# Products of C with the state on four tiles of 32 rows and 64 columns, in a chunked linear attention with two gated layers

## Chip, cores, metric

One core of one Trainium2 chip. The metric is the device time of one execution in microseconds; lower is better. Times that are shown for a kernel are the median of several executions, and one more execution was profiled.

## What is computed

x is [4, 8, 768, 32] (batch, heads, tokens, width), a is [4, 8, 768], B and C are [4, 8, 768, 16]. Cut to what matters, with chunks of tokens (the reference takes 32, the kernel 128; the result is the same sum):

```python
cum = cumsum(log(clip(a)))                          # in a chunk
L = exp(cum[i] - cum[j]) * (i >= j)
y_intra = ((C_i . B_j) * L) @ x                     # in a chunk
y_inter = (C @ state) * exp(cum)                    # from the chunks before
y = y_intra + y_inter
state = exp(sum(log_a)) * state + sum_j decay_j * B_j x_j
h = (sigmoid(y @ w_gate) * (y @ w_val)) @ w_out     # 256 -> 1536 -> 256
g = h @ w2_in                                       # 256 -> 2048
out = (g * sigmoid(g)) @ w2_out                     # 2048 -> 256
```

There is a state of 16 by 32 for each of the 8 heads of each batch. y of all heads, 256 wide, goes into the two gated layers, 3072 tokens in all.

## The kernel before, in words

The tokens are cut into 24 chunks of 128 (six for each batch), and the first gated layer takes them in blocks of 2, 2, 4, 4, 4, 4 and 4 chunks. The attention of later chunks is spread, in small steps, between the products of the first layer: `slot_steps(s)` (L407) lists what the attention does while chunk s is finished, and the loop at L642 takes some steps from the list after each gate, each value and each output product. While block b runs, the attention of block b+1 is computed. The order of the instructions of each engine is not written out: a planner sets it ahead of time from the order of the program and from the times that it reckons for each instruction, except for SyncE's queue, whose order is the program's. A tile with one buffer may be written anew once everything that reads its old content is done.

For a chunk q, with N = 16, D = 32, L = 128 tokens:

- `at_L` (L287) scans the decays on VectorE; `at_cb` (L321) makes C B in two halves of four heads (bank `cb`), and VectorE multiplies them by L (L337).
- `at_bw` (L297), on GpSimd, scales B and C by their decays into `bw` and `cw`. `at_cwT` (L312) transposes `cw` on TensorE into a bank `misc` (L317), and ScalarE copies it to SBUF (L319): `cwT`, [(head, n), token].
- `at_state` (L360) makes the sum of B x for a chunk: four pairs of heads, each a column tile of 32 columns (L368), into the same bank `misc`; VectorE adds it to the running state S2, [(head, n), (parity of the head, d)] (L377). `at_state2` (L382) writes the state as a block-diagonal matrix of 128 by 256 (L389), with zeros where row and column are of different heads.
- `at_y` (L339) builds y transposed, [(head, d), token], in one bank `y`, heads 0 to 3 in its columns 0 to 127 and heads 4 to 7 in columns 128 to 255. First come the two products of C with the state: for each half a full 128 by 128 tile of the block-diagonal matrix against `cwT` (L346); they start the sum. Then the eight products x L, one for each head, on a tile of 32 columns each (L352), four side by side. Chunks 0, 6, 12 and 18 start a batch and have no state product.
- `at_yT` (L395) splits y into hi and lo: a copy on ScalarE (L404), a subtraction on VectorE (L405), 256 columns each.

All of these are float32 products, which the trace shows as two records of weights and two of matmul each; the first layer's products (L462, L511) have tiles of 128 by 128 and 512 columns moving. In slots from 9 on, `joint` (L421) issues y of chunk s, both halves, then the transpose and the state sums of chunk s+1. PSUM has eight banks: three for gate and value, two for the first layer's sums, and one each for `misc`, `cb` and `y`.

After the attention its memory holds the second layer's weights, which are converted while the last block of the first layer runs (L676 to L678). At the start, `blk` (L100 to L103), a mask of 128 by 8, is made on GpSimd.

Of the kernel before, what the change touches and what calls it, by code (L numbers as in the profile page):

```python
# [8 lines left out]
F32 = mybir.dt.float32  # L9
# [9 lines left out]

# Tokens per block of the first gated layer, in chunks of 128.  # L20
BLOCKS = [2, 2, 4, 4, 4, 4, 4]
LAG = 2
# The first chunks, whose C B products take the short way through the tensor engine.
NX = 4
LB = 4
GV = 3
# Hidden blocks whose w_out is still whole for the first two blocks of tokens.
NAT = 7
# [5 lines left out]
def tile_linattn_moe_moe(  # L34
# [12 lines left out]
):  # L47
    """Decayed linear attention in chunks of 128, then two gated layers.

    float32 products run as float32r: an operand is split exactly into hi + lo  # L50
    (12 significant bits each) and hi*hi + hi*lo + lo*hi are summed in PSUM.
    The intra-chunk products split into three bfloat16 parts instead.

    The weights come as the raw 64-bit words of float64 and are rounded to float32
    (to nearest) on the chip.
    """
    nc = tc.nc
    nb, H, S, D = x.shape
    N = B.shape[-1]
# [13 lines left out]

# [1 line left out]
    wp = ctx.enter_context(tc.tile_pool(name="wp", bufs=1))  # L75
# [16 lines left out]

# [1 line left out]
    warm = wp.tile([P, 1], F32, name="warm")  # L94
# [3 lines left out]
    make_identity(nc, ident)  # L98
    # blk[(h n), h'] = 1 where h' == h
    blk = ap_.tile([P, H], F32, name="blk")  # L100
    nc.gpsimd.memset(blk, 1.0)
    nc.gpsimd.affine_select(blk, blk, [[-N, H]], ALU.is_ge, 0.0, base=0, channel_multiplier=1)
    nc.gpsimd.affine_select(blk, blk, [[N, H]], ALU.is_ge, 0.0, base=N - 1, channel_multiplier=-1)  # L103
    # eye[j, (h i)] = 1 where i == j
    eye = ap_.tile([P, H * L], BF16, name="eye")
    eye3 = eye.rearrange("p (h l) -> p h l", h=H)
    nc.vector.memset(eye, 1.0)
    nc.gpsimd.affine_select(eye3, eye3, [[0, H], [-1, L]], ALU.is_equal, 0.0, base=0, channel_multiplier=1)
    # sel[p, m] = 1 where p == L - 1
    sel = ap_.tile([P, P], F32, name="sel")  # L110
    nc.gpsimd.memset(sel, 1.0)
    nc.gpsimd.affine_select(sel, sel, [[0, P]], ALU.is_ge, 0.0, base=-(L - 1), channel_multiplier=1)

# [1 line left out]
    # exp of a sum of logs is a product: every decay is a running product of the  # L115
    # clipped a, which a scan over the tokens gives.
    def split(hi, lo, src):
        nc.scalar.copy(hi, src)
        nc.vector.tensor_sub(lo, src, hi.bitcast(F32))

# [1 line left out]
    # For each 128 of the hidden columns: hi and lo of [gate 2 x 128 | val 2 x 128 | out 256].  # L122
    w1 = w1p.tile([P, NF1, 2, 3 * DM], F32R, name="w1")
    cnt = 0

    def conv(raw, hi, lo, n, whole=None):
        """Raw float64 words [.., 2] -> float32, rounded to nearest, -> hi + lo;
        the last of them stay whole, if whole is given for them."""
        nonlocal cnt
        cnt += 1  # L130
        v = raw.rearrange("p (n t) -> p n t", t=2)
        t = stg["p"].tile([P, stg["n"]], F32, tag="cvt", name=f"cvt{cnt}", bufs=stg["cvt"])
        f, ti, r = t[:, :n], t[:, :n].bitcast(I32), v[:, :, 0]
        # The high word read as float32, times 2**-112, has the exponent field that
        # the float32 has after a shift by three bits; the sign is put back.
        nc.scalar.activation(f, v[:, :, 1].bitcast(F32), AF.Copy, scale=2.0**-112)
        nc.scalar.activation(r, v[:, :, 0].bitcast(U32), AF.Copy, scale=2.0**-29)
        nc.vector.tensor_scalar(ti, ti, 3, None, op0=ALU.logical_shift_left)  # L138
        nc.vector.scalar_tensor_tensor(  # L139
            ti, v[:, :, 1], -(2**31), ti, op0=ALU.bitwise_and, op1=ALU.bitwise_or  # L140
        )
        if whole is not None:
            n -= whole.shape[-1]
            nc.gpsimd.tensor_tensor(whole.bitcast(I32), ti[:, n:], r[:, n:], ALU.add)
            f, ti, r = f[:, :n], ti[:, :n], r[:, :n]
        nc.gpsimd.tensor_tensor(ti, ti, r, ALU.add)  # L146
        nc.scalar.copy(hi, f)
        nc.vector.tensor_sub(lo, f, hi.bitcast(F32))  # L148

    def load_w(w, f, ins, outs, native=None):  # L150
        """What the hidden columns f of a layer need of its weights."""
        nonlocal cnt
# [24 lines left out]
    def w1_split(f0, f1):  # L177
        """The whole w_out -> hi + lo."""
        for f in range(f0, f1):
            hi, lo = w1[:, f, 0, 2 * DM :], w1[:, f, 1, 2 * DM :]  # L180
            nc.scalar.copy(hi, whole(f))
            nc.vector.tensor_sub(lo, whole(f), hi.bitcast(F32))
# [3 lines left out]

# [1 line left out]
    T = [dict() for _ in range(NQ + 8)]  # L188

    def top(t):  # L190
        """The high halves of float32 words, as bfloat16."""
        return t.bitcast(BF16).rearrange("p (n t) -> p n t", t=2)[:, :, 1]
# [42 lines left out]
    def at_wide1(q):  # L235
# [7 lines left out]
        nc.scalar.copy(t["bT"], ps[:, :P])  # L243
        # C transposed, a copy for each head with zeros for the others
        t["cT"] = x1T[0][:, q % 2, q // 2 * H * L : (q // 2 + 1) * H * L].rearrange("p (h l) -> p h l", h=H)
# [19 lines left out]
    def at_bc3(q, which):  # L265
        """Parts 11122233 of B against parts 12312312 of C along the contraction."""
        t = T[q]
# [19 lines left out]
    def at_L(q):  # L287
        """L[j, h, i] = product of a over j < k <= i; 1 at i == j, 0 before.

        The scan restarts at i = 0, where a is replaced by 0."""  # L290
        t = T[q]
# [20 lines left out]
    def at_cwT(q):  # L312
        t = T[q]
        if q % NCH == 0:
            return
        ps = ps_at.tile([P, 512], F32, tag="misc", name=f"cwT{q}")
        nc.tensor.transpose(ps[:, :P], t["cw"].rearrange("p h n -> p (h n)"), ident)  # L317
        t["cwT"] = ap_.tile([P, P], F32, tag="cwT", name=f"cwT{q}", bufs=2)
        nc.scalar.copy(t["cwT"], ps[:, :P])  # L319

    def at_cb(q, half):  # L321
# [15 lines left out]
        nc.vector.tensor_mul(sl, ps, sl)  # L337

    def at_y(q, part):  # L339
        """y transposed, [(h d), i]: a head's 32 rows are a column tile."""  # L340
        t = T[q]
        if part == 0:
            t["y"] = ps_at.tile([P, KM, L], F32, tag="y", name=f"y{q}", bufs=1)
# [12 lines left out]

    # The state of a pair of heads, [(h n), (h' d)]: a column tile of 32 rows.
    S2 = ap_.tile([P, 2 * D], F32, name="S2")

    def at_state(q):  # L360
        b, c = divmod(q, NCH)
        t = T[q]
        if c == NCH - 1:
            return
        ps = ps_at.tile([P, 512], F32, tag="misc", name=f"st{q}")
        for p in range(H // 2):
            o = 2 * N * p
            nc.tensor.matmul(  # L368
                ps[o : o + 2 * N, : 2 * D],
                t["bw"][:, 2 * p : 2 * p + 2].rearrange("p h n -> p (h n)"),  # L370
                t["x"][:, 2 * p : 2 * p + 2].rearrange("p h d -> p (h d)"),
                start=True, stop=True, skip_group_check=True,
            )
        if c == 0:
# [7 lines left out]
    def at_state2(q):  # L382
        """The state as a block-diagonal matrix, [(h n), (h d)]."""
        t = T[q]
        if q % NCH == NCH - 1:
            return
        t["S"] = ap_.tile([P, DM], F32, tag="S", name=f"S{q}", bufs=2)
        sh = [P, H // 2, 2, D]
        nc.vector.tensor_mul(  # L389
# [5 lines left out]
    def at_yT(q):  # L395
        t = T[q]
        b, i = blk_of[q]
        if i == 0:
# [3 lines left out]
            ]  # L402
        hi, lo = (v[:, :, i * L : (i + 1) * L] for v in xT[b])
        nc.scalar.copy(hi, t["y"])  # L404
        nc.vector.tensor_sub(lo, t["y"], hi.bitcast(F32))  # L405

    def slot_steps(s, q0=0, q1=NQ):  # L407
        """What the attention does while chunk s is finished, as small steps;
        of chunks q0 to q1 only."""
        ok = lambda q: q0 <= q < q1  # L410
# [36 lines left out]

# [1 line left out]
    acc = {}  # L449
# [44 lines left out]
    def m1_out(b, f):  # L494
        n = BLOCKS[b] * L
        # Two blocks of at most 256 tokens can be under way, each in a bank.
        small = n <= 256
# [22 lines left out]

# [1 line left out]
    sp_order = ExitStack()  # L522
# [24 lines left out]

    # e_i[i, c, u]: the decay from the start of chunk c to its token i
    e_sb = first
# [10 lines left out]

    # dec[(h n), (c b)]: the decay over a whole chunk
    nc.tensor.matmul(
# [21 lines left out]

    # The weights are converted as the first two blocks run, these in turns.
    seen = set()
# [34 lines left out]

# [1 line left out]
    NA = 4  # L623
# [71 lines left out]

# [1 line left out]
    o2p = ctx.enter_context(tc.tile_pool(name="o2p", bufs=1))  # L697
# [93 lines left out]
    for o in queue_o[:-1]:  # L791
        m2_out(*o)
    # The last sums end one after the other, not all at once.
    with tc.manual_schedule(engines={mybir.EngineType.PE}):
# [32 lines left out]
```

## Time and profile before

| what | us |
|---|---|
| median of 3 executions | 680.7 (680.61 to 682.51) |
| span of the profiled execution, which is also the time on record for it | 680.8 |
| TensorE (matmul) busy | 647.7, 95% |
| TensorE (weight loads) busy | 524.9, 77% |
| VectorE busy | 436.0, 64% |
| ScalarE busy | 329.0, 48% |
| GpSimd busy | 109.3, 16% |

The span runs from the first to the last instruction. Busy times of different engines overlap, and the records of TensorE overlap each other as well: a matmul lasts longer than the distance to the start of the next. Line numbers are those of the kernel before. PE is TensorE, PEld its weight loads, DVE VectorE, ACT ScalarE, POOL GpSimd, SP SyncE.

### The profile page before, as it was taken

Reading aid. Unit: us, or ns where it says so; the run is one execution under the profiler, and the core shown is the slowest. Engines: PE = TensorE matmul, PEld = TensorE weight load, DVE = VectorE, ACT = ScalarE, POOL = GpSimd, SP = SyncE. Lnnn points to the kernel's source line nnn. Section 1 sums busy time; section 2 is a strip of 40 time slices with the busy share of each in tenths; the row PEclk is TensorE's granted clock in tenths of the full one; section 3 lists DMA queues with packets and bytes.
Section 4 is the critical chain, followed back from the end, with each engine's and each line's share of the span. In section 5 each row is a group of like instructions: output and inputs, shape, how many; then the busy total and the mean of one; then the engine's idle time right before and its main releaser. Section 6 shows DMA issues by size and latency. Waiting matters only on the chain.

```text
span 680.8 us, 10010 instructions
## 1 busy us (share of the span) xinstructions
PE 647.7 (95%) x3728; PEld 524.9 (77%) x3728; DVE 436.0 (64%) x658; ACT 329.0 (48%) x647; POOL 109.3 (16%) x128
## 2 busy tenths in 40 slices
PE   5689787999999999999999999999999999999997
PEld 2368676777777777777787888888888888888887
DVE  8987977767666758756689345464564555644544
ACT  5566634544444545435476335454454544534443
POOL 3534612212222313121133000000000000000000
PEclk9889989899999999999999999999999999999999
DMA  8935578867466375643132000000000000000000
GB/s 206 265 122 170 117 126 146 148 135 126 99 114 148 71 138 125 101 79 124 44 123 82 1 0 1 1 15 17 1 32 1 1 31 1 31 1 1 32 1 31
DMA packets 160592, 51.18 MB, mean 75 GB/s; under 512 B 119008, under 2 KB 156896, under 8 KB 160544
## 3 DMA queue, kind: packets, MB, share of 16 engines
q1 hardware_dynamic: 160544, 50.55, 33.4%
q8 instruction: 29, 0.48, 0.3%
q14 instruction: 19, 0.16, 0.1%
HBM read 36.80 MB, written 3.24 MB: 59 GB/s over the span
## 4 chain that ended last, share of the span: by engine, by line
PE 80%; DVE 6%; DMA 3%; issue 2%; POOL 2%; ACT 1%; SPq 1%; DVEq 0%; ACTq 0%; POOLq 0%
PE h L462 20%; PE acc L511 12%; PE v L462 12%; PE g L462 12%; PE o L739 11%; PE o L750 7%; PE o L745 2%; PE y L352 2%; PE cb L335 1%; DMA raw<-in_moe_w_out_dram 1%; DVE cvt L139 1%; PE y L346 1%; POOL cvt L146 1%; DVE cvt L138 1%; DVE w2b L148 1%
## 5 line engine op out<-in xcount | busy, mean ns | idle before, releaser
L462 PE MATMUL g<-xT,w 128*128 128x512 f32 (+1 forms) x504 | 124.2, 377 | 4.9 <-DVE sg L483 4.3
L462 PE MATMUL v<-xT,w 128*128 128x512 f32 (+1 forms) x504 | 121.7, 373 | 0.1
L462 PE MATMUL h<-x2T,w2b 128*128 128x512 f32 x432 | 113.3, 395 | 0.0
L719 DVE TENSOR_TENSOR sh<-h,sh 128x512 f32<-128x512 f32 x96 | 66.3, 691 | 69.6 <-ACT sh L718 69.0
L462 PEld LDWEIGHTS g<-xT,w 128*128 128x128 f32 x504 | 88.3, 193 | 24.3 <-DVE sg L483 5.5
L724 DVE TENSOR_TENSOR gl<-sh,gh 128x512 fp32r<-128x512 f32 x96 | 65.9, 691 | 55.5 <-ACT gh L456 31.9
L462 PEld LDWEIGHTS v<-xT,w 128*128 128x128 f32 x504 | 87.3, 191 | 17.0 <-issue 1.0
L511 PE MATMUL acc<-gh,w 128*128 128x512 f32 (+1 forms) x280 | 95.5, 384 | 1.6 <-ACT x1T L519 1.4
L718 ACT ACTIVATE sh<-h 128x512 f32<-128x512 f32 x96 | 57.7, 601 | 80.7 <-PE h L462 76.1
L462 PEld LDWEIGHTS h<-x2T,w2b 128*128 128x128 f32 x432 | 76.5, 188 | 15.2
L456 ACT CAST gh<-sh 128x512 fp32r<-128x512 f32 x96 | 59.2, 620 | 60.1 <-DVE sh L719 53.8
L456 ACT CAST gh<-sg 128x512 fp32r<-128x512 f32 (+1 forms) x70 | 41.2, 589 | 89.7 <-DVE sg L483 89.6
L739 PE MATMUL o<-w2b,gh 128*128 128x512 f32 x240 | 75.4, 395 | 0.0
L483 DVE TENSOR_TENSOR sg<-v,sg 128x512 f32<-128x512 f32 (+1 forms) x84 | 51.0, 607 | 30.0 <-PE v L462 29.8
L492 DVE TENSOR_TENSOR gl<-sg,gh 128x512 fp32r<-128x512 f32 (+1 forms) x70 | 50.1, 716 | 28.6 <-ACT gh L456 28.4
L295 DVE TENSOR_TENSOR_SCAN L<-L,eye 128x1024 f32<-128x1024 f32 x24 | 55.2, 2301 | 14.9 <-DMA L<-ac_d 14.6
L475 ACT ACTIVATE sg<-g 128x512 f32<-128x512 f32 (+1 forms) x84 | 44.9, 535 | 39.0 <-PE g L462 36.0
L511 PEld LDWEIGHTS acc<-gh,w 128*128 128x128 f32 x280 | 52.1, 189 | 13.1 <-ACT x1T L519 1.8
L750 PE MATMUL o<-w2b,gl 128*128 128x256 f32 x288 | 60.1, 280 | 0.0
L511 PE MATMUL acc<-gl,w 128*128 128x512 f32 (+1 forms) x140 | 53.9, 385 | 4.9 <-DVE gl L492 4.9
L146 POOL TENSOR_TENSOR cvt<-cvt,raw 128x512 int32<-128x512 int32 (+1 forms) x28 | 46.7, 1671 | 65.4 <-DVE cvt L139 50.6
L750 PEld LDWEIGHTS o<-w2b,gl 128*128 128x128 f32 x288 | 49.1, 188 | 4.9
(94 smaller groups left out, 784.9 us busy)
## 6 DMA issues: line engine op xcount, KB each, us to landing
L<-ac_d SPq DMA_DIRECT2D x23, 512.0 KB, 4.9
raw<-in_moe_w_out_dram SPq DMA_DIRECT2D x28, 256.0 KB, 3.7
raw<-in_moe_w_in_dram SPq DMA_DIRECT2D x16, 256.0 KB, 2.7
x<-in_x_dram SPq DMA_DIRECT2D x24, 128.0 KB, 2.8
raw<-in_moe_w_gate_dram SPq DMA_DIRECT2D x12, 256.0 KB, 4.3
raw<-in_moe_w_val_dram SPq DMA_DIRECT2D x12, 256.0 KB, 4.3
out_dram<-o2t SPq DMA_DIRECT2D x24, 128.0 KB, 1.8
bc<-in_B_dram SPq DMA_DIRECT2D x24, 64.0 KB, 2.8
```

Of the source, the lines that this page charges most:

```text
L146: nc.gpsimd.tensor_tensor(ti, ti, r, ALU.add)
L295: nc.vector.tensor_tensor_scan(t["Lf"], t["Lf"], eye, 0.0, op0=ALU.mult, op1=ALU.add)
L456: nc.scalar.copy(hi[:, :n], sg[:, :n])
L462: nc.tensor.matmul(psum[:, :n], w[:, i, o + k * P : o + (k + 1) * P], xt[j][:, k, :n], start=(z == 0), stop=(z == len(k_terms) - 1),)
L483: nc.vector.tensor_mul(sg[:, :n], ps[:, :n], sg[:, :n])
L492: nc.vector.tensor_sub(lo[:, :n], sg[:, :n], hi[:, :n].bitcast(F32))
L511: nc.tensor.matmul(o, v[:, ms], g[:, :n], start=(f == 0 and z == 0 and not (small and m)), stop=(f == NF1 - 1 and z == len(terms) - 1), sk ...
L718: nc.scalar.activation(sg, ps, AF.Sigmoid)
L719: nc.vector.tensor_mul(sg, ps, sg)
L724: nc.vector.tensor_sub(lo, sg, hi.bitcast(F32))
L739: nc.tensor.matmul(ps, hi[:, s], w2(f)[:, :, DM:], start=(f == 0), stop=False, skip_group_check=True,)
L750: nc.tensor.matmul(ps[:, :DM], lo[:, s], w2(f)[:, 0, DM:], start=False, stop=(f == NF2 - 1), skip_group_check=True,)
```

## The change

From chunk 9 on (`QT = 9`), the products of C with the state are four instead of two: each takes the 32 rows of one pair of heads and 64 columns, so nothing is multiplied with the zeros between pairs. They come behind the x L products of both halves and end the sum. The two halves of y lie in two banks, the ones of `y` and of `misc`. The transpose of C and the state sums of the next chunk go into free columns of these two banks, and TensorE is held to issue them behind the last product of y. The state is written with 64 columns instead of 256, with a mask `blk2` of two columns that is made once from `blk`. The copy of y and its subtraction become two of each, one for each bank. The docstrings and comments are taken out too, which changes nothing that runs.

```diff
+QT = 9
...
+    blk2 = ap_.tile([P, 2], F32, name="blk2")
+    nc.vector.tensor_reduce(blk2, blk.rearrange("p (a t) -> p t a", t=2), AX.X, ALU.add)
...
     def at_cwT(q):
...
-        ps = ps_at.tile([P, 512], F32, tag="misc", name=f"cwT{q}")
-        nc.tensor.transpose(ps[:, :P], t["cw"].rearrange("p h n -> p (h n)"), ident)
+        ps, order = behind(q, 0)
+        with order:
+            nc.tensor.transpose(ps[:, :P], t["cw"].rearrange("p h n -> p (h n)"), ident)
...
+    yb, y_end = {}, {}
+
+    def two_banks(q):
+        if q not in yb:
+            yb[q] = [ps_at.tile([P, 512], F32, tag=g, name=f"y{q}{g}", bufs=1) for g in ("y", "misc")]
+        return yb[q]
+
+    def behind(q, k):
+        if q <= QT:
+            return ps_at.tile([P, 512], F32, tag="misc", name=f"{('cwT', 'st')[k]}{q}"), nullcontext()
+        return two_banks(q - 1)[k][:, L:], tc.issue_after(y_end[q - 1].ins)
+
     def at_y(q, part):
         t = T[q]
+        if q >= QT:
+            t["y"] = [v[:, :L] for v in two_banks(q)]
+            for h in range(4 * part, 4 * part + 4):
+                o = D * (h % 4)
+                y_end[q] = nc.tensor.matmul(
+                    t["y"][part][o : o + D], t["x"][:, h], t["L"][:, h],
+                    start=True, stop=True, skip_group_check=True,
+                )
+            for p in range(H // 2) if part and q % NCH else ():
+                i, o = 2 * N * p, 2 * D * (p % 2)
+                y_end[q] = nc.tensor.matmul(
+                    t["y"][p // 2][o : o + 2 * D], T[q - 1]["S"][i : i + 2 * N], t["cwT"][i : i + 2 * N],
+                    start=False, stop=True, skip_group_check=True, tile_position=(i, o),
+                )
+            return
...
     def at_state(q):
...
-        ps = ps_at.tile([P, 512], F32, tag="misc", name=f"st{q}")
-        for p in range(H // 2):
+        ps, order = behind(q, 1)
+        with order:
+            for p in range(H // 2):
...
     def at_state2(q):
...
+        if q + 1 >= QT:
+            two = lambda v: v.rearrange("p (t d) -> p t d", t=2)
+            t["S"] = t["S"][:, : 2 * D]
+            nc.vector.tensor_mul(two(t["S"]), two(S2), blk2.unsqueeze(2).to_broadcast([P, 2, D]))
+            return
...
     def at_yT(q):
...
+        if q >= QT:
+            for m in range(KM):
+                nc.scalar.copy(hi[:, m], t["y"][m])
+                nc.vector.tensor_sub(lo[:, m], t["y"][m], hi[:, m].bitcast(F32))
+            return
```

## Rows read from the trace of the kernel before

**Rows 1.** The page: busy times, and TensorE's busy share in 40 slices.
```profile
PE 647.7 (95%) x3728; PEld 524.9 (77%) x3728; DVE 436.0 (64%) x658; ACT 329.0 (48%) x647; POOL 109.3 (16%) x128
...
PE   5689787999999999999999999999999999999997
```

**Rows 2.** Busy time by stretch: stretch, us, then PE, PEld, DVE, ACT, POOL; clock; DMA.
```profile
122.00:336.00 214.00, 214.00 (x1316) 165.82 (x1315) 144.04 (x223) 97.24 (x200) 45.03 (x59) 1.00 0.56 110
```

**Rows 3.** State products: whole span (ns min/median/max, first to last start); group from 125 to 336 us.
```profile
L346 PE MATMUL y<-cwT,S x80: 270/275/422, 19.4 to 325.4; 128*128 128x128 f32 x80
...
L346 PE MATMUL y<-cwT,S 128*128 128x128 f32 x52 | 8.1, 277 | 0.0
```

**Rows 4.** Timeline of TensorE, chunk 14: start us, us to last end, instruction, count.
```profile
201.33 0.86 PE L462 MATMUL v<-xT,w 128*128 128x512 f32 x3
202.02 0.60 PE L346 MATMUL y<-cwT,S 128*128 128x128 f32 x4
202.56 0.65 PE L352 MATMUL y<-L,x 128*32 128x128 f32 x16
203.13 0.33 PE L317 MATMUL cwT<-ident,cw 128*128 128x128 f32 x1
203.30 0.39 PE L335 MATMUL cb<-tr,tr 128*128 128x128 bf16 x4
```

**Rows 5.** Timeline of TensorE, chunk 16: state products between large tiles.
```profile
233.00 0.61 PE L346 MATMUL y<-cwT,S 128*128 128x128 f32 x4
233.37 1.64 PE L462 MATMUL g<-xT,w 128*128 128x512 f32 x6
```

**Rows 6.** Timeline of TensorE, chunk 16: y products entered from a large tile.
```profile
237.41 0.39 PE L511 MATMUL acc<-gh,w 128*128 128x512 f32 x1
237.73 0.65 PE L352 MATMUL y<-L,x 128*32 128x128 f32 x16
238.31 0.33 PE L317 MATMUL cwT<-ident,cw 128*128 128x128 f32 x1
```

**Rows 7.** Timeline of TensorE: the state sums on their own.
```profile
195.80 0.86 PE L462 MATMUL v<-xT,w 128*128 128x512 f32 x3
196.59 0.32 PE L368 MATMUL st<-x,bw 128*32 128x64 f32 x8
196.84 0.40 PE L335 MATMUL cb<-tr,tr 128*128 128x128 bf16 x4
```

**Rows 8.** Timeline of TensorE: chunk 9, whose y comes in two pieces.
```profile
138.94 0.66 PE L346 MATMUL y<-cwT,S 128*128 128x128 f32 x4
139.53 0.43 PE L352 MATMUL y<-L,x 128*32 128x128 f32 x8
139.89 0.33 PE L317 MATMUL cwT<-ident,cw 128*128 128x128 f32 x1
...
144.58 0.43 PE L352 MATMUL y<-L,x 128*32 128x128 f32 x8
144.82 0.29 PE L368 MATMUL st<-x,bw 128*32 128x64 f32 x8
```

**Rows 9.** Timeline of TensorE: six transposes of 32 rows at the start.
```profile
5.75 0.84 PE L554 MATMUL ps_e<-ident,x1T 32*128 32x32 f32 x6 [0.60 <-DVE x1T L550]
6.55 1.22 PE L329 MATMUL cb<-x1T,bT 128*128 128x512 f32 x1
```

**Rows 10.** Split of y, 125 to 336 us: count, busy us, mean ns, idle before.
```profile
L405 DVE TENSOR_TENSOR xT<-y,xT 128x256 fp32r<-128x256 f32 x16 | 6.7, 418 | 6.2 <-ACT xT L404 6.1
L404 ACT CAST xT<-y 128x256 fp32r<-128x256 f32 x16 | 5.9, 368 | 1.9 <-PE y L352 1.7
```

**Rows 11.** VectorE: timeline of the start; and its only reduction (ns).
```profile
2.12 0.70 DVE L528 MEMSET x1T<- 32x768 f32 x1
2.98 0.62 DVE L201 TENSOR_SCALAR x1T<-x1T 32x768 f32<-32x768 f32 x1 [0.15 <-DMA x1T<-in_a_dram]
...
L572 DVE TENSOR_REDUCE dec<-dtmp x1: 354/354/354, 11.7 to 11.7; 128x24 f32<-128x192 f32 x1
```

**Rows 12.** Timeline of TensorE: the idle time behind the attention.
```profile
366.19 0.50 PE L511 MATMUL acc<-gh,w 128*128 128x512 f32 x1 [1.38 <-ACT x1T L519]
```

More of the change, by code (lines that the diff above doesn't have):

```diff
@@ L1 @@
-from contextlib import ExitStack
+from contextlib import ExitStack, nullcontext
 import concourse.bass as bass
@@ L364, in at_state @@
             return
-        ps = ps_at.tile([P, 512], F32, tag="misc", name=f"st{q}")
-        for p in range(H // 2):
[L367 to L373, printed above, removed]
+        ps, order = behind(q, 1)
+        with order:
+            for p in range(H // 2):
+                o = 2 * N * p
+                nc.tensor.matmul(
+                    ps[o : o + 2 * N, : 2 * D],
+                    t["bw"][:, 2 * p : 2 * p + 2].rearrange("p h n -> p (h n)"),
+                    t["x"][:, 2 * p : 2 * p + 2].rearrange("p h d -> p (h d)"),
+                    start=True, stop=True, skip_group_check=True,
+                )
         if c == 0:
```

## The prediction

> **What bounds the kernel now.** I read the page first, for the busy shares and the granted clock. TensorE is busy 95% of the span, and of the 40 slices only the first third shows it short of work [rows 1]. An average over unlike stages says little, so the next view was the table of stretches [rows 2]. From 122 to 336 us TensorE is busy for all of the 214.00 us, at a granted clock of 1.00 (the 2.4 GHz level). The change acts on chunks 9 to 23, whose products with the state lie between 138.9 us [rows 8] and 325.4 us [rows 3], all of them in this stretch; over its 14 steps that is some 13 us a chunk. There a microsecond taken from TensorE's row of work is a microsecond of the span, and one taken from any other engine is nothing.
>
> Busy time of a group is a poor price here, since matmuls overlap: the 52 records of the state products in this stretch hold 8.1 us busy, but nothing idle before them [rows 3]. So the third view was the timeline of TensorE, read by the start of one group to the start of the next. In a joined chunk the four records of C with the state (each float32 product is two records) start at 202.02 and the y products at 202.56, which is 0.54 us; the sixteen y records then take 0.57 us to the transpose [rows 4]. Where the same four records stand alone among 128 by 128 tiles they take 0.37 us [rows 5]. The other 0.17 us is the passage to the tiles of 32 columns. Nine of the thirteen state products from chunk 9 on (13 to 17 and 19 to 22) belong to chunks whose y records run in one piece; in four (9, 10, 11, 23) they run in two pieces some 5 us apart [rows 8].
>
> **The change part by part.** *The products themselves.* Removed: 0.54 us a chunk of four records. Added: eight records of 32 rows and 64 columns. The trace has no such tile. The nearest rows are half a y: eight records on four tiles side by side take 0.36 us up to the next 128 by 128 group [rows 8]; the moving side has 128 columns there as here. I take 0.36. Since y now comes first, it is y that is entered from the stream: before a y that stands alone the last large matmul takes 0.32 us to the next start instead of 0.23, three of which fill 0.69 [rows 4, 6], so 0.09 is added. Between y and the new tiles I keep the passage that y has today to a 128 by 128 group (0.58 us for the sixteen [rows 6]). A joined chunk so goes from 0.54 + 0.57 to 0.09 + 0.58 + 0.36, that is 1.11 to 1.03 us: 0.08 gained, 0.7 us over nine chunks.
>
> The passage from tiles of 32 columns to tiles of 32 rows by 64 columns is the unknown that matters. From y to the state sums, both tiles of 32 columns, eight records take 0.24 us instead of 0.36 [rows 8], so a passage that costs nothing would give back 0.12 us each time. From above I bound it by the 0.17 us between 128 by 128 and 32 columns [rows 4, 5], which is 0.05 us more than the 0.12. I take the price in full, because the shape of the tile changes here and the free row keeps it.
>
> The Trainium skill, "TensorEngine Tiling (Array Packing)", section "Tiling Modes" under "Key Properties", says that a change of the tiling mode drains the engine while a change of tile does not; that speaks against this change, which puts one more mode into each chunk. By that rule the sum is the one I take; by the 0.24 us row it would be some 1.8 us lower. The trace agrees with the rule where 128 by 128 meets 32 columns (0.17 us [rows 4, 5]), and no row has the third shape.
>
> *Chunks in two pieces.* Four of them. The first two tiles of the state need only the first half of y, so the order that is worked out ahead may set them behind each half: 2 x 0.36 + 0.09 against the 0.59 us of today's group [rows 8], a loss of 0.22 us. If all four wait for the second half it is 0.36 + 0.09 against 0.59, a gain of 0.14. Nothing in the trace says which; I take the middle, +0.04 x 4 = +0.2 us, and keep -0.6 and +0.9 for the range.
>
> *The state sums and the transpose of C.* They move behind the state products into the free columns of y's banks, and the sums no longer wait for ScalarE to empty the bank that they shared with the transpose. Their eight records cost the same; what differs is the entry. Today they are entered from the stream (0.79 us for three large matmuls, where 0.69 is three [rows 4, 7]), later from the transpose, whose next start is 0.17 us off [rows 4]. That entry is between free and 0.09 us dearer than the 0.17, so the gain is 0 to 0.09 for each of eleven: I take half, -0.5 us. Behind the pair TensorE holds cb of the next chunk; it starts later by the sums' 0.25 us [rows 7] and is wanted a chunk later, some 13 us on.
>
> *ScalarE and VectorE.* The copy of y out of PSUM and its subtraction become two of half the size, the block-diagonal state shrinks from 256 columns to 64. Today's copy takes 0.37 us and the subtraction 0.42 [rows 10]. If the half ones cost as much as the whole, that is 0.37 + 0.42 us a chunk more at worst, 15 chunks, 5.6 us on ScalarE and 6.3 on VectorE, less the saving on the state. I cost them at nothing: in this stretch ScalarE is busy 97.24 and VectorE 144.04 of 214.00 us [rows 2], and no TensorE group waited for either [rows 3]. Without that cover the bound would be those 6 us.
>
> *The bank of the sums.* y of the next chunk now needs the sums to have been read out. They stand behind the previous y, a whole chunk earlier, so this wait has most of 13 us of slack and costs nothing.
>
> *The small mask, once.* One reduction on VectorE at the start, of 8 columns. It stands before the clearing of 768 columns at 2.12 us, behind which there is only 0.15 us of idle time before the decays [rows 11]. Its price is between nothing and the 0.35 us of the larger reduction [rows 11]: I take 0.2, on the path.
>
> **The sum.** -0.7 + 0.2 - 0.5 + 0.2 = -0.8 us. The profiled execution has a span of 680.8 us, 0.1 above the median of 680.7, so the sum may be set against either: **679.8 us** with the small rounding left in. What a measurement of this kernel can tell from no change is about 0.3%, 2.0 us: 678.7 to 682.7.
>
> **The rivals.** *The passage is free* (y's tiles and the new ones count as one shape). For: from y to the sums it is [rows 8]. Against: there the shape is the same. Nine joined chunks and about six passages in the four split ones, 15 x 0.12 = 1.8 us: 678.0.
>
> *The tiles run one after another; this is the one on the slower side.* The only records of 32 rows in the trace, six transposes at the same place in the array, start 0.80 / 6 = 0.13 us apart [rows 9]. Eight like that are 1.04 us where I have 0.24 without the passage: 0.8 x 13 = 10.4 us, 690.2. For: no row shows two row positions side by side. Against: four column positions do run side by side, eight records in 0.24 us [rows 8]. It decides from (2.0 + 0.8) / 13 = 0.22 us more per product.
>
> *Two of the four wait for each other.* The products of heads 0 to 3 write one bank, from two row positions. If the second waits, there are four steps in place of two, as in a whole y against a half: 0.58 - 0.36 = 0.22 us [rows 6, 8], times 13 is 2.9, 682.7. For it speaks that only two banks serve four tiles; against it that they write different partitions of it, as y's four tiles do [rows 8]. The Trainium skill, on the same page under "Gotcha 1: PSUM Pressure", says that different row tiles can't use one bank at once; nothing in the trace of before shows it.
>
> *The wait behind the attention.* TensorE stands idle 1.38 us before 366.19 until ScalarE has copied the first layer's sums [rows 12]. By the code, ScalarE also converts the second layer's weights then, into memory that the attention gives up with its last y; so the last y sets part of what ScalarE has in front of that copy. If the shifted order takes this wait away, 678.4; if it doubles, 681.2.
>
> **How the numbers follow.** The sum as worked out: 0.46. The free passage: 0.20. The wait at 366 us gone: 0.09. Two waiting for each other: 0.10. One after another: 0.07. The wait doubled or some chunk's order worse than taken: 0.08. Faster by over 0.3% are the free passage and the vanished wait and a little of the first case: 0.30. Slower are the serial tiles, half of the pairs' case and some of the last: 0.15. The rest, 0.55, can't be told from no change. The range of 677.0 to 682.8 us reaches from the free passage with a good order in the split chunks (678.0 less 0.6 and a part of the sums' other half gain) to the pairs' case; the serial tiles, and free passage and vanished wait together (676.6), are left out, under 2 in 10.
>
> **What would show it.** In the changed trace a joined chunk should read large matmul to y 0.32 us, y 0.58, new tiles 0.36. If y to the new tiles is 0.46, the passage is free. If the new tiles take 0.58 or 1.16, they wait for each other. The stretch from 122 to 336 us should stay at full busy time and end about 1 us earlier, with the granted clock at 1.00; the idle time before 366 us should still be between 1 and 2 us. The forecast is wrong if idle time appears on TensorE between 122 and 336 us, for then a wait and not its row of work decides.

## The result, and the profile after

The changed kernel takes 687.29 us (median of 6 runs) where the kernel before took 681.61 beside it: a ratio of 1.0089, with a 95% interval of 1.0073 to 1.0105. It is 0.9% slower, 5.7 us; the forecast was 679.8, and no measurable difference the likeliest. The profiled execution has a span of 685.7 us, 4.9 more than before. (An execution's time is some 1.7 us over its span: 681.35 and 679.6 in the first experiment below. The span of before of 680.8 so belongs to an execution somewhat above the median, not at it, as the text ahead had it; the difference is too small to matter here.)

The busy line of the page and the stretch that the change acts on, to be set beside [rows 1, 2]:

```profile
PE 656.1 (96%) x3780; PEld 523.5 (76%) x3780; DVE 432.9 (63%) x674; ACT 329.7 (48%) x662; POOL 102.4 (15%) x128
...
122.00:336.00 214.00, 214.00 (x1333) 157.84 (x1332) 139.10 (x228) 94.61 (x208) 36.96 (x58) 1.00 0.54 109
```

TensorE is still busy for all of the 214 us, at a granted clock of 1.00, and VectorE and ScalarE have a little less to do there than before. No other engine became the bound, and no wait appeared: TensorE simply has more to do. How much more is read where the second layer begins, behind the attention. Each kernel's first products for it (first and last start at the end of the line), before and after:

```profile
L462 PE MATMUL h<-x2T,w2a x144: 387/389/402, 405.6 to 637.1; 128*128 128x512 f32 x144
```

```profile
L511 PE MATMUL h<-x2T,w2a x144: 387/389/402, 410.5 to 642.0; 128*128 128x512 f32 x144
```

They start 4.9 us later, and from there on the two kernels run alike. The idle 1.38 us of [rows 12] is gone as well: in the timeline after, the same first sums of the last block follow the product before them without a wait.

```profile
369.73 1.66 PE L511 MATMUL v<-xT,w 128*128 128x512 f32 x6
371.23 0.40 PE L560 MATMUL acc<-gh,w 128*128 128x512 f32 x1
```

So TensorE's row of work grew by about 4.9 + 1.4 = 6.3 us in the attention. Counted from the same product in both (the 41st of 512 columns, at 133.10 us before and 132.88 after) to the second layer, and without idle time, it is 271.12 us before and 277.57 after. This measure, called the row below, serves for the experiments too. The timeline of one chunk that runs in one piece (chunk 19) shows that it isn't the price of the products themselves:

```profile
280.87 0.40 PE L560 MATMUL acc<-gh,w 128*128 128x512 f32 x1
281.20 0.42 PE L367 MATMUL y19y<-L,x 128*32 128x128 f32 x8
281.44 0.40 PE L367 MATMUL y19misc<-L,x 128*32 128x128 f32 x8
281.77 0.33 PE L374 MATMUL y19y<-cwT,S 32*64 32x128 f32 x2
281.78 0.32 PE L374 MATMUL y19misc<-cwT,S 32*64 32x128 f32 x2
...
282.15 0.33 PE L323 MATMUL y19y<-ident,cw 128*128 128x128 f32 x1
282.41 0.32 PE L406 MATMUL y19misc<-x,bw 128*32 128x64 f32 x8
```

A large product to y 0.33 us, y 0.57, state products 0.38: nearly to the hundredth what the forecast had (0.32, 0.58, 0.36). But few chunks look like this. Chunk 13, whose y ran in one piece before, and chunk 16, of which single heads now stand alone between large products:

```profile
191.12 0.43 PE L367 MATMUL y13y<-L,x 128*32 128x128 f32 x8
191.47 0.43 PE L374 MATMUL y13y<-cwT,S 32*64 32x128 f32 x4
191.84 0.73 PE L511 MATMUL v<-xT,w 128*128 128x512 f32 x2
192.50 0.42 PE L367 MATMUL y13misc<-L,x 128*32 128x128 f32 x8
192.85 0.43 PE L374 MATMUL y13misc<-cwT,S 32*64 32x128 f32 x4
193.22 0.33 PE L323 MATMUL y13y<-ident,cw 128*128 128x128 f32 x1
193.48 0.32 PE L406 MATMUL y13misc<-x,bw 128*32 128x64 f32 x8
193.73 0.40 PE L341 MATMUL cb<-tr,tr 128*128 128x128 bf16 x4
...
228.57 0.41 PE L367 MATMUL y16y<-L,x 128*32 128x128 f32 x2
228.91 0.50 PE L560 MATMUL acc<-gh,w 128*128 128x512 f32 x1
229.34 0.41 PE L367 MATMUL y16y<-L,x 128*32 128x128 f32 x2
```

Two of the four tiles take 0.37 us with their passage out (191.47 to 191.84), as much as all four in chunk 19 (0.38). Counted through the timeline, y of chunks 9 to 23 runs in 30 pieces where it ran in 19, and the state products in 21 where they ran in 13. The view of the state products' line says the same: the weight loads stood idle before them 21 times, 0.20 us each, for no releaser, which is the passage.

```profile
its engine sat idle before it (us, times) until:
  issue: 4.2, 21
```

The sum: 8 more pieces of state products at 0.37 are 3.0 us. A cut in y costs two waves' extra way out (two halves 2 x 0.36 against one of 0.58 is 0.14), an entry of 0.09, and 0.09 by which the large product behind it starts its next one later (228.91 lasts 0.50 where 0.40 is usual): 0.32 us, and 11 more are 3.5. Together 6.5 us against the 6.3 read off above and the 6.45 by the row. It is an estimate, which leaves out what the chunks that stayed whole gained.

### The profile page after: what moved, and what is told of

The parts are those of the page before. It is cut to its first block, busy times and chain, and to the rows that moved or that the text cites. A ratio compares the mean times of both kernels' runs of the same rounds, so it can differ in the third digit from the quotient of the medians.

```text
span 685.7 us, 10144 instructions
## 1 busy us (share of the span) xinstructions
PE 656.1 (96%) x3780; PEld 523.5 (76%) x3780; DVE 432.9 (63%) x674; ACT 329.7 (48%) x662; POOL 102.4 (15%) x128
## 4 chain that ended last, share of the span: by engine, by line
PE 81%; DVE 4%; DMA 4%; ACT 2%; POOL 2%; issue 1%; SPq 1%; DVEq 0%; POOLq 0%; ACTq 0%
PE h L511 19%; PE acc L560 12%; PE g L511 12%; PE v L511 12%; PE o L788 11%; PE o L799 7%; PE o L794 2%; DMA raw<-in_moe_w_out_dram 2%; DMA L<-ac_d 2%; PE cb L341 1%; POOL cvt L151 1%; DVE L L300 1%; DVE cvt L144 1%; ACT cvt L141 1%; DMA bc<-in_C_dram 1%
## 5 line engine op out<-in xcount | busy, mean ns | idle before, releaser
L541 DVE TENSOR_TENSOR gl<-sg,gh 128x512 fp32r<-128x512 f32 (+1 forms) x70 | 51.8, 740 | 34.1 <-ACT gh L505 33.7
```

Source lines behind the costliest of these rows:

```text
L541: nc.vector.tensor_sub(lo[:, :n], sg[:, :n], hi[:, :n].bitcast(F32))
```

## The experiments

Three theories were set against each other. A: the tiles cost what was forecast, and the time went into the pieces. B: the tile of 32 rows and its passage cost more than the full tiles. C: something else of the change, such as the mask or the split of y. Each ratio below is to the kernel before on the same chip.

**e1_joined.** y starts with its second half, and TensorE is held to the order.

```diff
-                at_y(q, 0)
-                at_y(q, 1)
+                with tc.manual_schedule(engines={mybir.EngineType.PE}):
+                    at_y(q, 1)
+                    at_y(q, 0)
...
-            for p in range(H // 2) if part and q % NCH else ():
+            for p in range(H // 2) if not part and q % NCH else ():
```

> The changed kernel with one thing altered: the y products are issued with the second half first, then the first half, then the four state products, and TensorE is held to that order; so y starts when the later of its two banks is free and runs in one piece. Theory A (pieces: the new tiles are priced as forecast, and the time went into y and the state products being cut into more pieces, each with its own entry and exit): y falls from 30 pieces to about 17 and the state products from 20 to 12; with 0.32 us for an entry, 0.20 us for an exit and 0.2 us for a passage that takes some 6.5 us from TensorE's row of work between 122 and 336 us, and the time is 681 us, give or take the 1.4 us of the wait near 366 us, so level with the kernel before. Theory B (tiles: the tile of 32 rows by 64 columns and its passage cost more than the two full tiles): 685 us or more, since every chunk keeps them. Theory C (the rest of the change, such as the mask or the split of y): 685 us or more.

Measured: 681.96 us, ratio 0.9999 (0.9984 to 1.0014). All of the loss is gone, with the small tiles in every chunk that has a state product. y runs in 17 pieces and the state products in 13. Chunk 13 in its timeline:

```profile
194.32 0.43 PE L367 MATMUL y13misc<-L,x 128*32 128x128 f32 x8
194.56 0.40 PE L367 MATMUL y13y<-L,x 128*32 128x128 f32 x8
194.89 0.33 PE L374 MATMUL y13y<-cwT,S 32*64 32x128 f32 x2
...
195.27 0.33 PE L323 MATMUL y13y<-ident,cw 128*128 128x128 f32 x1
```

From y to the transpose it is 0.95 us, where the changed kernel needs 2.10 with two large products between the halves. A holds; B and C fall.

**e2_one_release.** The sums lie beside the transpose in the first bank.

```diff
-        return two_banks(q - 1)[k][:, L:], tc.issue_after(y_end[q - 1].ins)
+        return two_banks(q - 1)[0][:, (1 + k) * L :], tc.issue_after(y_end[q - 1].ins)
```

> The changed kernel with one thing altered: the state sums of the next chunk lie in the first of the two banks, beside the transpose, in place of the second; no order is forced. So the second bank is free as soon as y has been read, and the first is the later one for both halves. Theory A with its cause (the halves come apart because the second bank, with the sums in it, comes free later than the first): y falls from 30 pieces to about 21 and the state products from 20 to 15, while the sums stand alone again; 4.9 us less on TensorE than the changed kernel, about 682.5 us. If the banks are not the cause of the pieces: no change, 687 us. Theory B: 686 us or more.

Measured: 682.23 us, 1.0010 (0.9996 to 1.0024), as theory A had it, with y in 21 pieces and without any order being forced. In its timeline the sums of chunk 13 run apart, 6 us ahead of y, and are read out only at 190.15 us (L415), just before the second product of C B with L (L343); then both halves of y start together:

```profile
186.27 0.32 PE L406 MATMUL y12y<-x,bw 128*32 128x64 f32 x8
...
190.15 0.27 DVE L415 SCALAR_TENSOR_TENSOR S<-S,dec,y12y 128x64 f32<-128x64 f32 x1
190.34 0.68 DVE L343 TENSOR_TENSOR L<-cb,L 128x512 f32<-128x512 f32 x1
...
192.04 0.43 PE L367 MATMUL y13misc<-L,x 128*32 128x128 f32 x8
...
192.28 0.40 PE L367 MATMUL y13y<-L,x 128*32 128x128 f32 x8
```

The first bank, which chunk 13 takes over, was last read until 191.96 us (L451), 0.08 us before the halves start. That leaves two readings: the sums had held the second bank, or they now hold the first one back until the second half is ready too. A later run (e11) parts them.

**e3_off.** QT = 24, so that of the change only the mask is left.

```diff
-QT = 9
+QT = 24
```

> The changed kernel with QT = 24, so that no chunk takes the new way; what stays of the change is the small mask at the start. Theories A and B: the time of the kernel before, 681.6 us, within 1 us. Theory C in its part of the mask and the start: 683 us or more.

Measured: 682.50 us, 1.0001 (0.9982 to 1.0020). The mask costs nothing that can be measured.

**e4_full_tiles.** The full tiles of before, ahead of y, in the changed kernel.

```diff
+            for m in range(KM) if not part and q % NCH else ():
+                nc.tensor.matmul(
+                    t["y"][m], T[q - 1]["S"][:, m * P : (m + 1) * P], t["cwT"],
+                    start=True, stop=False, skip_group_check=True,
+                )
             for h in range(4 * part, 4 * part + 4):
...
-                    start=True, stop=True, skip_group_check=True,
+                    start=(q % NCH == 0), stop=True, skip_group_check=True,
...
-            for p in range(H // 2) if part and q % NCH else ():
...
-        if q + 1 >= QT:
+        if q + 1 >= 99:
```

> The changed kernel with the state products as before: two full tiles, ahead of the y products, over the state with 256 columns; the two banks, the transpose and the sums behind y, and the split in halves stay. No tile of 32 rows is left. Theory A: the two banks alone cut y into about 24 pieces where the kernel before has 19, and cost 1.9 us on TensorE: 683 to 684 us, slower than before though no new tile is there; the rest up to 687 us is the state products being cut and the passages that each piece of them has. Theory B: 681 to 682 us, the time of before, since the tiles at fault are gone.

Measured: 685.48 us, 1.0057 (1.0036 to 1.0078). Without one small tile it is slower than before: the two banks, with the transpose and the sums in them, cut y into 24 pieces by its timeline, as A had expected. In chunk 13 a single large product stands between the halves:

```profile
192.91 0.43 PE L372 MATMUL y13y<-L,x 128*32 128x128 f32 x8
193.27 0.51 PE L509 MATMUL v<-xT,w 128*128 128x512 f32 x1
193.70 0.43 PE L372 MATMUL y13misc<-L,x 128*32 128x128 f32 x8
```

The time is 1.5 us above what A had expected. The row is 273.1 us, 2.0 more than before, and A had 1.9. In the profiled execution, the longest of the six, the first large product of 512 columns starts 2.3 us later than before (121.9 against 119.6 us), ahead of the stretch in question; what does that was not followed up.

**e5_state_products_joined.** The order is held, but with the first half first.

```diff
-                at_y(q, 0)
-                at_y(q, 1)
+                with tc.manual_schedule(engines={mybir.EngineType.PE}):
+                    at_y(q, 0)
+                    at_y(q, 1)
```

> The changed kernel with TensorE held to the order first half of y, second half, state products; the halves may still come apart, but the state products no longer do. Theory A: the state products fall from 20 pieces to 12 and y from 30 to 26; by the prices of the trace (0.36 to 0.38 us for a piece of state products with its passages, however many of the four it holds) 4.4 us less on TensorE than the changed kernel, 1.6 us more than the kernel before: 682 to 683.5 us, that is, two thirds of the loss is in the state products being cut. If the pieces of y alone carried the loss: 685 to 686 us.

Measured: 683.86 us, 1.0028 (1.0011 to 1.0045): 0.6% of the 0.9% come back when the state products alone are joined, while y still runs in 26 pieces. It is a little above the expected 683.5, within what the interval allows (682.8 to 685.1 on 682.03).

**e6_sums_before_transpose.** As e1, with two lines exchanged.

```diff
-                    at_cwT(q + 1)
-                    at_state(q + 1)
+                    at_state(q + 1)
+                    at_cwT(q + 1)
```

> As e1_joined, and the state sums are issued ahead of the transpose of C instead of behind it. Theory A by the rows: from the transpose to the sums it is 0.26 us and from the sums onward 0.15, while from the state products to the sums it is 0.20 and from the sums to the transpose should be about 0.15; 1.1 us less on TensorE than e1_joined, 1.9 less than the kernel before: 680 us where the kernel before has 681.8. If the wait near 366 us grows by what TensorE gains before it: 681 to 682 us.

Measured: 680.41 us, 0.9969 (0.9953 to 0.9985), faster than both kernels. Sums and transpose together take 0.41 us up to C B (192.50 to 192.91), where the changed kernel takes 0.51 (193.22 to 193.73): 0.26 from the transpose to the sums and 0.25 from there. The row is 269.25 us, 1.9 less than before, as A had it.

```profile
192.50 0.32 PE L406 MATMUL y13misc<-x,bw 128*32 128x64 f32 x8
192.75 0.33 PE L323 MATMUL y13y<-ident,cw 128*128 128x128 f32 x1
192.91 0.39 PE L341 MATMUL cb<-tr,tr 128*128 128x128 bf16 x4
```

**e7_joined_ahead.** As e6, with y and its state products at a higher priority.

```diff
-                with tc.manual_schedule(engines={mybir.EngineType.PE}):
+                with tc.high_priority(), tc.manual_schedule(engines={mybir.EngineType.PE}):
```

> As e6_sums_before_transpose, and y and its state products have a higher priority than the first layer's products, so that no head is left alone ahead of the others: y in 15 pieces, one a chunk, state products in 12. Theory A: 3.3 us less on TensorE than the kernel before, 678.5 us, faster than both kernels; if the wait behind the attention takes a part of it back, 679 to 681 us. Theory B does not allow less than 685 us with the new tiles in every chunk.

Measured: 682.05 us, 0.9988 (0.9973 to 1.0003): a miss. y is in 15 pieces as meant, and the row is 268.7 us, 0.6 less than in e6. But the other priority also changes the order ahead of chunk 9. In the profiled execution, 1.4 us above the median, TensorE waits 4.00 us there for GpSimd's scaled B (between 100 us and there its longest wait was 2.31 us before), and the stretch begins 3 us late. In e8, with the same priority, that wait was 2.62 us and the stretch began at 119.7 us, as before, and e8 is no faster. So the late start is not shown to be the whole of the miss.

```profile
121.63 0.44 PE L406 MATMUL st<-x,bw 128*32 128x64 f32 x8 [4.00 <-POOL bw L308]
```

**e8_joined_ahead_full_tiles.** As e7, with e4's full tiles, the second one first.

```diff
-            for m in range(KM) if not part and q % NCH else ():
+            for m in (1, 0) if part and q % NCH else ():
```

> As e7_joined_ahead, but with the two full tiles of the kernel before in place of the four of 32 rows, ahead of y. It tells what the small tiles are worth when the order is good. By the rows, full tiles that stand in the stream of large products cost 0.36 us and no passage, four small ones 0.18 and a passage of 0.2: the same within 0.5 us of e7_joined_ahead. If the small tiles are worth the 0.08 us a chunk that was forecast: 1 us slower than e7_joined_ahead. If they are the fault (theory B): 5 us faster.

Measured: 681.98 us, 0.9996 (0.9982 to 1.0011), the same as e7, and a row of 269.1 us. With the same order, small and full tiles can't be told apart.

**e9_full_tiles_sums_first.** e8 without the priority, so e6 with full tiles.

```diff
-                with tc.high_priority(), tc.manual_schedule(engines={mybir.EngineType.PE}):
+                with tc.manual_schedule(engines={mybir.EngineType.PE}):
```

> As e6_sums_before_transpose, but with the two full tiles ahead of y in place of the four of 32 rows behind it; the second half of y still comes first and TensorE is still held to the order. If the small tiles are what makes e6 faster than the kernel before: about 1 us slower than e6, level with before. By theory A and the prices of the rows (a pair of full tiles in the stream of large products 0.36 us, without a passage; y in 15 pieces) the small tiles are worth nothing: 1.7 us less on TensorE than e6, 679 to 680.5 us, and what makes both faster than before is the order of the pieces alone.

Measured: 677.75 us, 0.9943 (0.9921 to 0.9966). It is the fastest kernel of the study, 0.6% under the kernel before and below the 679 to 680.5 us that A had expected; the row is 267.50 us, 1.75 less than in e6, and A had 1.7. The full tiles go into the stream of large products or behind C B and pay no passage, and y, sums and transpose follow in one go:

```profile
188.33 0.40 PE L341 MATMUL cb<-tr,tr 128*128 128x128 bf16 x4
188.56 0.44 PE L366 MATMUL y13misc<-cwT,S 128*128 128x128 f32 x2
188.84 0.39 PE L366 MATMUL y13y<-cwT,S 128*128 128x128 f32 x2
...
194.06 0.43 PE L372 MATMUL y13misc<-L,x 128*32 128x128 f32 x8
194.31 0.40 PE L372 MATMUL y13y<-L,x 128*32 128x128 f32 x8
194.52 0.29 PE L404 MATMUL y13misc<-x,bw 128*32 128x64 f32 x8
194.75 0.33 PE L323 MATMUL y13y<-ident,cw 128*128 128x128 f32 x1
```

So what makes e6 and e9 faster than before is the order of the pieces and the two banks that allow it, not the small tiles.

**e10_products_twice.** e6 with each state product issued twice, so that the products with the state are added twice to y.

```diff
-            for p in range(H // 2) if not part and q % NCH else ():
+            for p in (0, 1, 2, 3, 0, 1, 2, 3) if not part and q % NCH else ():
```

> As e6_sums_before_transpose, with the four state products of each chunk issued twice, one set behind the other; the products with the state are so added twice to y. It measures the tile itself without a passage. Tiles side by side, as forecast (half of a y is two waves of 0.11 us): 0.22 to 0.25 us for each of 13, about 3 us slower than e6, 683 to 684 us. One after another (0.13 us each): 13 us slower, 693 us. Two of the four waiting for each other: 0.45 us each, 6 us slower, 686 us.

Measured: 681.36 us, 0.9989 (0.9977 to 1.0002), 0.2% or 1.4 us above e6's ratio; the expected 3 us lie within the two intervals. The timeline is plainer: eight more records add two steps of 0.11 us, to 0.60 us from 0.38. The row is 271.7 us, 2.5 more than in e6, where 13 times the 0.22 us are 2.9.

```profile
193.67 0.33 PE L374 MATMUL y13y<-cwT,S 32*64 32x128 f32 x2
...
193.83 0.27 PE L374 MATMUL y13y<-cwT,S 32*64 32x128 f32 x2
...
193.94 0.28 PE L374 MATMUL y13y<-cwT,S 32*64 32x128 f32 x2
...
194.05 0.27 PE L374 MATMUL y13y<-cwT,S 32*64 32x128 f32 x2
...
194.27 0.32 PE L406 MATMUL y13misc<-x,bw 128*32 128x64 f32 x8
```

All four tiles run side by side. The rival of serial tiles and that of two waiting for each other both fall.

**e11_banks_exchanged.** The transpose in the second bank, the sums in the first.

```diff
-        return two_banks(q - 1)[k][:, L:], tc.issue_after(y_end[q - 1].ins)
+        return two_banks(q - 1)[1 - k][:, L:], tc.issue_after(y_end[q - 1].ins)
```

> The changed kernel with one thing altered: the transpose lies in the second bank and the state sums in the first, the other way round; no order is forced. In e2 the sums shared the first bank with the transpose, had to wait for its copy, and came late, so e2 leaves open why the halves join. If the second half comes apart because the sums in its bank are read out late: the halves join here too, 682 us. If it is the other thing that the second half waits for, the second half of C B times L on VectorE, and e2 joined them only because its sums held the first bank back: the pieces stay, 30 of y, and the time is that of the changed kernel, 687 us.

Measured: 687.65 us, 1.0077 (1.0057 to 1.0098), as slow as the changed kernel, with y in 30 pieces and the same cut:

```profile
191.31 0.42 PE L367 MATMUL y13y<-L,x 128*32 128x128 f32 x8
191.66 0.43 PE L374 MATMUL y13y<-cwT,S 32*64 32x128 f32 x4
192.03 0.96 PE L511 MATMUL v<-xT,w 128*128 128x512 f32 x3
192.92 0.43 PE L367 MATMUL y13misc<-L,x 128*32 128x128 f32 x8
```

So it is not the bank in which the sums lie. The second half comes apart from the first in whichever bank, and the reason that A had given in e2, the sums in the second bank, falls; e2 joined them by holding the first bank back. That the second half waits for the second product of C B with L is what is left in the code; it was not tried by itself. On the chip, in the changed kernel, that product was not late for chunk 13:

```profile
190.04 0.69 DVE L343 TENSOR_TENSOR L<-cb,L 128x512 f32<-128x512 f32 x1
```

It ended at 190.73 us, and the second bank was last read at 184.16 (L451), both before even the first half starts at 191.12. So nothing on the chip kept this second half back until 192.50; the order set ahead of time did. In chunk 9 it was late: it ended at 141.00, behind the first half's start at 138.81, and that chunk came in two pieces before the change too.

## Why the prediction was wrong

**The step that failed is the count of the pieces.** The forecast took it from the trace of before that nine joined chunks stay joined and four come in two, and it priced a cut for those four alone, at +0.22 us at worst and +0.04 in the sum. After the change only chunks 18, 19 and 21 ran whole: 30 pieces of y where there were 19, 21 of the state products where there were 13, and 6.3 us more on TensorE. Two things in the change itself undid the old count, and both stood in the text; they are read from the code. The state products had come first, in the same bank as all of y, so no head could start before them; now they come last, and a head can start as soon as its own bank and its half of L are there. And y in one bank had one release for both halves; in two banks each half has its own. The counts agree: with the state products in front again and the two banks kept (e4), y runs in 24 pieces, five more than before and six fewer than in the changed kernel. The planner takes what it reckons to be ready, and nothing in its order shows that it reckons with the passages: it puts one head between two large products (chunk 16). Why it sets the second half of a chunk apart where everything was there in time (chunk 13) stays open. The rival "some chunk's order worse than taken" shared its 0.08 with the doubled wait and had no price of its own, and the range allowed +0.9 us for the four chunks alone; it came to 6.3 us, while the range ended at 682.8, with the pairs' case.

**Right: the prices.** A joined chunk as worked out (1.03 us) came out at 0.95 from y to the transpose plus an entry of 0.10. The passage from 32 columns to 32 rows by 64 is not free: from y to the new tiles it is 0.57 us (281.20 to 281.77), where a free one would have read 0.46, and the weight loads stand idle 0.20 us in it. I had taken it in full, and that held. The Trainium skill's "TensorEngine Tiling (Array Packing)", under "Key Properties", says that a change of the tiling mode drains the engine. The trace agrees, with 21 idle stretches of 0.20 us. The same page of the Trainium skill says under "Gotcha 1: PSUM Pressure" that different row tiles can't access one PSUM bank at the same time. The trace differs, and the measurement decides: the two tiles of one bank, on different partitions of it, start within 0.01 us of each other, and doubling them adds no more than the steps of 0.11 us (e10). Tiles on the same partitions were not run.

**Right: the bound.** TensorE was never idle between 122 and 336 us, at a clock of 1.00, before as after, so its row of work decided. ScalarE's and VectorE's doubled copies cost nothing.

**Too kind by half a microsecond: sums and transpose.** I had taken -0.5 us, halfway to a free entry. From the transpose to the sums it is 0.26 us, against 0.17 to C B before and 0.09 for the entry from the stream: no gain. The gain was there in the other order (e6, 0.10 us a chunk). The mask's +0.2 was nothing that can be measured (e3). Even uncut, the change would have gained nothing that shows: with the order held (e1) the row is 270.5 us, 0.6 less than before, and two pieces of y fewer than before make that up (2 x 0.32, an estimate).

**The wait behind the attention** did go away (1.38 us), as one rival had it, and hid a part of the loss: 6.3 us more work appear as 4.9 in the span.

**The serial tiles** gave a number near the result (690.2), but for another reason; the timeline and e10 exclude them.

## What to carry to other kernels

Where a planner sets the order, a change that gives parts of a product their own release, or that moves the part that held the rest together, changes how often a group is cut; price a cut (entry, exit, and the large product behind it: 0.3 to 0.4 us here) and count how many groups can now be cut, not how many were. A group that should stay whole is begun with the part that is ready last and held in its order: that alone took the 0.9% back here. Then ask again what the new instruction is worth; with the same order, two full tiles without a passage were as good as four small ones, or better.

## What the runs showed of the hardware

Two tiles of 32 rows by 64 columns take as long as four: 0.37 us with the passages for two (191.47 to 191.84), 0.38 for four. The way out of half a y, with 128 columns moving, was the same to another narrow shape and to a full tile: its eight records took 0.35 us to the state products (191.12 to 191.47) and 0.36 to a transpose [rows 8], some 0.20 of it behind the last record's start. Behind the sums, with 64 columns moving, the transpose starts 0.25 us after the first of them (e6), and the eight need 0.10 of that, which leaves 0.15. From a transpose it is 0.26 us to the narrow tiles of the sums (193.22 to 193.48) and 0.17 to a full one [rows 4].
